# A planned attention and two-MoE kernel: transfers planned as one queue, by rows and bytes

## The chip, the cores and the metric

The kernel runs on one core of a Trainium2 chip. The metric is the device time of one execution in microseconds (us). The engines are named PE (TensorE, matmul and transposes), DVE (VectorE), ACT (ScalarE), POOL (GpSimd) and SP (SyncE, which only issues transfers here).

## What is computed

Causal attention with a gate bias over 4 batches, 8 heads, 576 positions and head size 64; then a first MoE layer (512 to 1024 to 512) with a softmax-weighted and normalized middle; then a second one (512 to 2048 to 512) with a clipped middle. There are 2304 tokens.

```python
scores = scale * np.matmul(q, k.transpose(0, 1, 3, 2))
cum = np.cumsum(np.maximum(s, 0.0), axis=-1)
bias = -(cum[:, :, :, None] - cum[:, :, None, :])
scores = np.where(causal, -1000000000.0, scores + np.minimum(bias, 0.0))
attn = softmax(scores)
x = np.matmul(attn, v)                      # heads side by side: 2304 x 512
h = x @ w_in
solu = h * softmax(h)
x = (solu - mean(solu)) / sqrt(var(solu) + 1e-06) * g_ln @ w_out
h = x @ w2_in
out = (h * np.clip(h + 3.0, 0.0, 6.0) / 6.0) @ w2_out
```

## The kernel before

All large products run on PE in a fast 32-bit form, each operand split into a high and a low part, so that one product takes three matmuls. The weights arrive as 64-bit words: a load (`raw_wi`, `raw_wo`, `rawi`, `rawo`) is decoded by ACT (`a_`: high word), by ACT or DVE (`t_`: low word) and by DVE (joined), and then split.

The attention goes by pairs of heads. For each query tile PE makes scores (L782 for the first batch, L818 later), DVE takes the maximum (L727), ACT the exponential with its row sum (L739), DVE the reciprocal, POOL scales the rows of `y` (L834, L852), PE transposes them (L886), ACT and DVE copy these into `pt` (L890), and PE multiplies with v (L913). The first MoE goes by tiles of 128 tokens (L1018, L1087, L1108) and stores its output in memory. The second MoE is a Strassen-like scheme: 24 units (3 token blocks, 8 column pairs) of seven products (L1358), whose results ACT copies into `c` (L1371) and gates with a ReLU into `g` (L1384), which is stored in memory; then nine groups of seven products (L1535) with weights `W` that are loaded into `stage` and cast (L1445) and with `r` read back (forms `fa`, `fs`, L1512). `ws` is the split form of the input weights of one unit column (L472).

No loop sets the order in which instructions stand. The functions call `plan.add(engine, us, fn, reads, writes, new, lag, ...)`, and the class `Plan` keeps a list of work. `emit` then plays it through: each engine takes, when it comes free, the ready entry that was added first (entries in the background get a rank 50 or 100 later); an entry is ready when all that it reads is written, with a hop of 0.2 or 0.3 us between engines. PSUM banks are handed out there too. The entries are then emitted in the order of their planned starts, and each engine runs its own in just that order, whatever happens.

A transfer is an entry of SP, ACT or POOL that lasts as long as its issue; what it writes counts as ready `lag` later, a number by kind: 2.0 us for decoded weights on SP, 4.0 for those that ACT issues, 4.5 for `g`, 2.5 for `W`, 3.0 for `xr`, and so on. However many transfers are on their way, each has its own lag. After the first batch `plan.spare` adds a cushion to each planned duration: 0.03 us on DVE, 0.05 on ACT, none on POOL.

Of the kernel before, what the change touches and what calls it, by code (L numbers as in the profile page):

```python
# [41 lines left out]
TRIO = 3  # L42
X_RAW = 2
HOP_TO_PE, HOP_FROM_PE, HOP = 0.3, 0.2, 0.2


class Plan:


    def __init__(self):  # L50
        self.ops, self.writers, self.users, self.rings, self.born, self.reuse = [], {}, {}, {}, {}, []
        self.takes, self.bank = {}, {}
        self.stage, self.stages = "", {}
# [43 lines left out]
    def emit(self):  # L97
# [20 lines left out]
        for i, o in enumerate(self.ops):  # L118
# [3 lines left out]
            if not waits[i]:  # L122
                heapq.heappush(pending[o[0]], (0.0, i))
        order, port_free = [], 0.0
        while len(order) < n:
# [19 lines left out]
            if i in self.takes:  # L145
# [51 lines left out]
def kernel(ctx, tc, q, k, v, s, w_in, w_out, g_ln, w2_in, w2_out, out):  # L197
    nc = tc.nc
# [80 lines left out]
    def gate_rows():  # L279
# [37 lines left out]
        for i in range(len(blocks)):  # L317
            plan.add("ACT" if i >= 2 else "SP", 0.45, lambda i=i: load(i), writes=[f"s/{i}"], lag=2.0)
        plan.add("DVE", 0.55, lambda: nc.vector.memset(one, 1.0), writes=["one"])
# [8 lines left out]
        def to_dram():  # L328
            plan.add("POOL", 0.6, lambda: nc.gpsimd.tensor_scalar(neg, first_t["cum"][: 2 * NH].bitcast(F32), -1.0, 1.0, ALU.mult, ALU.mult), reads=["gate/h", "gate/l1"], writes=["neg"])
            for x in range(2):  # L330
                r = blocks[x]
                for i, row, src, keys in ((0, 2 * x, lambda r: one[:NH], ["one"]), (1, 2 * x + 1, lambda r: one[:NH], ["one"]), (1, 2 * x, lambda r: first_t["cum"][r].bitcast(F32), ["gate/h", "gate/l1"]), (0, 2 * x + 1, lambda r: neg[r], ["neg"])):
                    plan.add("SP", 0.45, lambda i=i, row=row, src=src, r=r: put(i, row, src(r)), reads=keys, writes=[f"rows/{i}{row}"], lag=4.0)

# [12 lines left out]
    def split64(plan, pool, src, hi, lo, name, key, scale=None, bufs=1, ring="", raws64=2, after=(), hi_dve=False, on_dve=(), on_act=(), behind=None, needs=(), home=()):  # L347
# [44 lines left out]
        def put_lo():  # L392
# [3 lines left out]
            else:  # L396
# [22 lines left out]
    def decoded(pool_at, x, k, tags, ready):  # L419
# [6 lines left out]
        def block(o):  # L426
# [54 lines left out]
    def second_w2(k, pool_at, tags, stage, ready=None):  # L481
# [4 lines left out]
        def whole(i, q):  # L486
            def go():
                nc.sync.dma_start(out=wt_d[i, :, k], in_=quarters()[q])

            return lambda: plan.add("SP", 0.6, go, reads=[both[q // 2]], writes=[f"wt{k}/{i}"], lag=3.0)  # L490

        def parts(i, m, q, tag):
# [9 lines left out]
            return part(at, lambda x: T[key][:, :, x, :], key, new=[(tag[1], 1, key)], alloc=alloc) + [  # L502
                lambda: plan.add("SP", 0.6, store, reads=[f"{key}/{x}{at[0]}" for x in "hl"], writes=[f"wt{k}/{i}"], lag=4.0)]

# [61 lines left out]
    def load_qk(p):  # L566
# [7 lines left out]
        for name, src in (("q", q), ("k", k)):  # L574
# [4 lines left out]
            elif p == X_RAW:  # L579
                new, room = ([("x", 2, "x0")], []) if name == "q" else ([], ["x0/raw"])  # L580
            plan.add("SP", 1.1, lambda name=name, src=src: rows(name, src), reads=room, writes=[key], new=new, lag=4.0)

# [4 lines left out]
    def load_v(p, a=1):  # L587
# [11 lines left out]
        for j in range(2):  # L599
            plan.add("SP", 0.5 + 0.5 * a, lambda j=j: values(j), writes=[f"{key}/{j}"], new=[("V", 2, key)] if j == 0 else [], lag=3.0, after=[begun(p)])  # L600

# [51 lines left out]
    def prep_qk(p, name):  # L653
# [47 lines left out]
        def to_stack(j):  # L701
            if p == NPAIR and name == "q":
                plan.add("POOL", 1.3, lambda j=j: zeros(j), writes=[f"stack{j}/"], new=[(f"stack{j}", 1, f"stack{j}")])
            s_key = f"S{p}_{j}"
            plan.add("SP", 1.26, lambda j=j: stack(j), reads=[f"{hl_key}/{x}{c0}" for x in "hl" for c0, _ in groups] + [f"stack{j}/"],
                     writes=[f"{s_key}/{name}"], new=[(f"S{j}", 1, s_key)] if name == "q" else [], lag=3.0)
            if name == "k":
                plan.add("SP", 0.45, lambda j=j: gates(j), reads=ROWS_D + [f"stack{j}/"], writes=[f"{s_key}/g"], lag=2.0)

# [392 lines left out]
    def ffn1_out(c, m):  # L1102
# [18 lines left out]
        plan.add("ACT", act(256), put, reads=[key], writes=[f"so{key}/"])  # L1121
        plan.add("SP", 0.5, store, reads=[f"so{key}/"], writes=[f"x2_{c}_{m}"], lag=2.0)

# [72 lines left out]
    to_dram()  # L1196
    plan.add("SP", 0.5, lambda: nc.sync.dma_start(out=g_sb, in_=g_ln.rearrange("(c p) -> p c", p=P)), writes=["g"], lag=2.0, after=["HL0k/h0"])
    for b, share in enumerate(SHARES):
        main = []
        if b == 0:  # L1200
# [72 lines left out]
    def load_x(bi, lows):  # L1273
# [72 lines left out]
    def unit(bi, k):  # L1346
# [32 lines left out]
        def gate(o, h, src_key, src, eng="DVE"):  # L1379
# [44 lines left out]
    def weights(j):  # L1424
# [4 lines left out]
        for q, (k0, k1) in enumerate(PIECES):  # L1429
# [25 lines left out]
            if i in SPLIT:  # L1455
                r.append(lambda both=both, key=key, k0=k0, k1=k1, number=number: plan.add(
                    "SP", 0.0032 * 2 * P * (k1 - k0), both, reads=[f"wt{k}/{WT_PART[i]}" for k in range(k0, k1)], writes=[f"{key}/h", f"{key}/l"], new=[(f"rm{number}", 1, key)], lag=2.5))
                continue
            r += [
                lambda load=load, key=key, k0=k0, k1=k1, first=["stage"] * (number == 0), ring=[("xr", 1, "stage")] * (number == 0) + [(f"stage{home}" if home in (0, 1) else home, 1, f"{key}s")]: plan.add(  # L1460
                    "SP", 0.0016 * 2 * P * (k1 - k0), load, reads=[f"wt{k}/{WT_PART[i]}" for k in range(k0, k1)], writes=[f"{key}s", *first], new=ring, after=["stage"], lag=2.5),
                lambda high=high, key=key, n=n, number=number: plan.add("ACT", act(n), high, reads=[f"{key}s"], writes=[f"{key}/h"], new=[(f"rm{number}", 1, key)]),
# [9 lines left out]
    def group(bi, t):  # L1472
# [16 lines left out]
        def load(x, h, o):  # L1489
# [3 lines left out]

            return lambda: plan.add("SP", 1.6, go, reads=[f"gd{bi}_{h}{o}/{k}" for k in range(NK)] + (["forms"] if mine[x] == 4 else []), writes=[key(x)], new=raw_new(x), lag=3.5)

# [52 lines left out]
        def put(b, h, o, kept):  # L1548
# [10 lines left out]
            def store():  # L1559
# [90 lines left out]
```

## Time and profile before

| what | value |
|---|---|
| median of 3 runs | 799.75 us (799.14 to 799.86) |
| the profiled execution | 798.7 us, of it span 796.9 us |
| PE busy | 771.1 us (97%) |
| DVE, ACT, POOL busy | 595.1 us, 478.2 us, 228.3 us |
| DMA | 136.33 MB, mean 171 GB/s |

The span runs from the first to the last instruction. A busy share says how long an engine had an instruction in it; in a row of waits stands how long an engine stood idle before a group of instructions and what ended it. In a timeline each row is an instruction or a run of equal ones, with the idle time ahead of it in brackets. Line numbers are those of the kernel before.

### The profile page before, as it was taken

How to read it: one execution, taken by the hardware profiler on the slowest of the kernel's cores; microseconds unless marked ns; L12 is line 12 of the kernel's file. 1: busy time of each engine (PE TensorE's matmuls, PEld its weight loads, DVE VectorE, ACT ScalarE, POOL GpSimd, SP SyncE). 2: the span in 40 equal slices, each digit the busy share in tenths (PEclk: the TensorE clock that was granted, in tenths of full speed). 3: DMA queues.
4: the chain of work that ended last, by engine and by line, in shares of the span. 5: the costliest groups of instructions: out<-in, count | busy, mean ns of one | idle time of the engine just before them, and what ended most of it. 6: DMA issues, size and time to landing. Idle time of an engine off the chain costs nothing.

```text
span 796.9 us, 15897 instructions
## 1 busy us (share of the span) xinstructions
PE 771.1 (97%) x5560; PEld 707.0 (89%) x5560; DVE 595.1 (75%) x1381; ACT 478.2 (60%) x1071; POOL 228.3 (29%) x320
## 2 busy tenths in 40 slices
PE   6889999999999999999999999999997999999997
PEld 5566888888898988888989999999997999999997
DVE  5767988778957688657798898888876876666662
ACT  5877987757765667656374665666664444444441
POOL 3575454436642455251210000000032002222221
PEclk9879999999999999999999999999999999999999
DMA  8856688777757776613433545666599444444440
GB/s 204 204 141 160 162 208 202 196 195 198 169 171 194 212 170 157 187 51 139 142 107 108 183 166 175 211 218 234 167 294 412 152 140 133 131 134 131 132 128 27
DMA packets 157615, 136.33 MB, mean 171 GB/s; under 512 B 67616, under 2 KB 135200, under 8 KB 157536
## 3 DMA queue, kind: packets, MB, share of 16 engines
q1 hardware_dynamic: 153600, 122.07, 53.6%
q10 hardware_dynamic: 2400, 8.54, 3.4%
q0 software_dynamic: 1536, 4.72, 1.5%
q8 instruction: 44, 0.72, 0.4%
q14 instruction: 35, 0.29, 0.1%
HBM read 74.67 MB, written 39.39 MB: 143 GB/s over the span
## 4 chain that ended last, share of the span: by engine, by line
PE 80%; DMA 7%; DVE 6%; ACT 3%; issue 2%; POOL 1%; SPq 1%; DVEq 0%; ACTq 0%; POOLq 0%
PE bank L1535 23%; PE bank L1358 18%; PE bank L1108 10%; PE bank L1018 8%; PE bank L913 6%; PE bank L886 5%; PE bank L818 5%; PE bank L782 2%; DMA stage<-wt_d 2%; DMA rawo<-in_moe_w_out_dram 2%; DMA xr<-x_d 2%; PE bank L1087 1%; PE bank L667 1%; DMA rawi<-in_moe_w_in_dram 1%; DMA raw_wi<-in_moe_w_in_dram 1%
## 5 line engine op out<-in xcount | busy, mean ns | idle before, releaser
L1358 PE MATMUL bank<-xb,ws 128*128 128x384 f32 x1008 | 178.1, 337 | 4.5 <-ACT c L1371 3.4
L1358 PEld LDWEIGHTS bank<-xb,ws 128*128 128x128 f32 x1008 | 175.1, 188 | 6.2 <-ACT c L1371 4.6
L1535 PE MATMUL bank<-W,fs 128*128 128x256 f32 x864 | 106.3, 282 | 0.3 <-ACT c L1544 0.3
L1535 PEld LDWEIGHTS bank<-W,fs 128*128 128x128 f32 x864 | 104.3, 190 | 0.6 <-ACT c L1544 0.5
L834 POOL TENSOR_SCALAR y<-y,rsum 128x128 f32<-128x128 f32 (+4 forms) x120 | 72.5, 623 | 98.2 <-DVE rsum L830 84.9
L727 DVE CUSTOM_DVE_ANT_0 y<-bank,mask 96x288 f32<-96x288 f32 (+4 forms) x168 | 74.2, 466 | 26.2 <-PE bank L818 21.4
L739 ACT ACTIVATE y<-y,nmax 128x128 f32<-128x128 f32 (+4 forms) x140 | 83.1, 595 | 14.4 <-DVE nmax L727 7.2
L1108 PE MATMUL bank<-zh,w_out_h 128*128 128x256 f32 x288 | 83.1, 289 | 0.7 <-DVE zl L1094 0.7
L1535 PE MATMUL bank<-W,fa 128*128 128x256 f32 x648 | 81.2, 282 | 2.0 <-ACT fa L1512 1.5
L1535 PEld LDWEIGHTS bank<-W,fa 128*128 128x128 f32 x648 | 78.9, 190 | 2.6 <-ACT fa L1512 1.7
L1108 PE MATMUL bank<-zh,w_out_l 128*128 128x256 f32 x288 | 81.0, 281 | 0.0
L1108 PE MATMUL bank<-zl,w_out_h 128*128 128x256 f32 x288 | 80.9, 281 | 0.0
L1392 POOL DMA_DIRECT2D g_d<-g x24 | 13.2, 551 | 189.0 <-DVE g L1387 189.0
L1018 PE MATMUL bank<-w_in_h,xh 128*128 128x512 f32 x144 | 60.2, 418 | 0.0
L818 PE MATMUL bank<-stack 128*96 128x288 f32 (+4 forms) x288 | 58.6, 318 | 0.0
L1108 PEld LDWEIGHTS bank<-zh,w_out_h 128*128 128x128 f32 x288 | 54.2, 188 | 2.7 <-DVE zl L1094 1.2
L1018 PE MATMUL bank<-w_in_h,xl 128*128 128x512 f32 x144 | 56.6, 393 | 0.0
L1018 PE MATMUL bank<-w_in_l,xh 128*128 128x512 f32 x144 | 56.4, 392 | 0.0
L1512 ACT CAST fs<-r 128x1024 fp32r<-128x1024 f32 x27 | 28.4, 1050 | 44.8 <-PE bank L1535 27.7
L1108 PEld LDWEIGHTS bank<-zh,w_out_l 128*128 128x128 f32 x288 | 54.3, 188 | 0.4
L886 PE MATMUL bank<-ident,y 128*128 128x128 f32 (+2 forms) x420 | 52.3, 265 | 2.3 <-POOL y L852 2.3
L1108 PEld LDWEIGHTS bank<-zl,w_out_h 128*128 128x128 f32 x288 | 54.3, 188 | 0.0
(275 smaller groups left out, 1575.7 us busy)
## 6 DMA issues: line engine op xcount, KB each, us to landing
r<-g_d SPq DMA_DIRECT2D x36, 512.0 KB
g_d<-g SPq DMA_DIRECT2D x72, 192.0 KB
rawo<-in_moe_w_out_dram SPq DMA_DIRECT2D x16, 512.0 KB
rawi<-in_moe_w_in_dram SPq DMA_DIRECT2D x16, 512.0 KB
x_d<-x2s SPq DMA_DIRECT2D x36, 128.0 KB
xr<-x_d SPq DMA_DIRECT2D x6, 768.0 KB
g_d<-g POOLq DMA_DIRECT2D x24, 192.0 KB, 5.5
W<-wp_d SPq DMA_DIRECT2D x6, 768.0 KB
```

The costliest lines, as they stand in the source:

```text
L727: nc.vector.tensor_tensor_reduce(out=ys[h, t][:n, c0:c1], in0=bank(key)[:n, : c1 - c0], in1=mask[:n, 480 + n - w + c0 : 480 + n - w + c1], ...
L739: nc.scalar.activation(out=y[:n], in_=y[:n], func=AF.Exp, bias=nmax[:n, h, t : t + 1], scale=-1.0, accum_out=sums[:n, h, t : t + 1])
L782: nc.tensor.matmul(bank(keys[j])[:n, : c1 - c0], lhsT=a, rhs=b, start=(m == 0), stop=(m == 3))
L818: nc.tensor.matmul(bank(key)[:n, : c1 - c0], lhsT=ss[:, 2 - 2 * m, ST[t] : w], rhs=ss[:, 3 - 2 * m, c0:c1], start=(m == 0), stop=(m == 1))
L834: nc.gpsimd.tensor_scalar(ys[h, t][:n], ys[h, t][:n], rsum[:n, h, t : t + 1], 1.0, ALU.mult, ALU.mult)
L886: nc.tensor.transpose(bank(key)[: SZ[jj], c : c + SZ[t]], ys[h, t][: SZ[t], ST[jj] : ST[jj] + SZ[jj]], ident[: SZ[t], : SZ[t]])
L913: nc.tensor.matmul(bank(key)[j * D : (j + 1) * D, lo - c0 : c1 - c0], lhsT=vs[v_key(p, a)][:n, jj, j, :], rhs=pts[pt_key(2 * p + j, a)][:n ...
L1018: nc.tensor.matmul(bank(key), lhsT=xs[i][m // 2][:, kk, :], rhs=(w_in_l if m == 1 else w_in_h)[:, kk, f * 512 : (f + 1) * 512], start=(kk ...
L1108: nc.tensor.matmul(bank(key)[:, : 2 * P], lhsT=w_out_at(w, kk)[:, m * P : (m + 1) * P], rhs=z[:, kk, :], start=(kk == 0 and i == 0), stop= ...
L1358: nc.tensor.matmul(bank(key)[:, :W], lhsT=T[f"ws{k}"][:, WS_OF[op], a, kc * P : (kc + 1) * P], rhs=x_form(bi, op)[:, b, kc, :], start=(fir ...
L1512: nc.scalar.copy(T[name][:, 0], T[key(src)])
L1535: nc.tensor.matmul(bank(b_key)[:, : 2 * P], lhsT=T[name][:, y, k, :], rhs=T[f"W{i}_{q}"][:, k - k0, w, :], start=first and k == 0 and y == ...
```

## The change

The list gets a model of one queue in which all transfers stand. An entry may carry `dma`, the time that its transfer holds the queue, in place of `lag`; it is worked out from the number of rows (pieces in memory) and their size. In `emit` a transfer begins 1.3 us after its issue has ended, or when the one before it is through, whichever is later; it holds the queue for `dma`, and what it writes is ready 0.3 us after that. All three issuing engines share the one queue. The cushion after the first batch goes from 0.03 and 0.05 us to 0.01 and 0.02. Line numbers below L44 rise by 1, later by 9.

```diff
+DMA_START, DMA_END = 1.3, 0.3
...
-            us, lag = self.ops[i][1], self.ops[i][4]
+            us, landed = self.ops[i][1], self.ops[i][4]
...
             free[e] = end = start + us
+            if self.dma[i]:
+                dma_free = max(end + DMA_START, dma_free) + self.dma[i]
+                landed = dma_free + DMA_END - end
...
-                ready_at[j] = max(ready_at[j], end + lag + hop if done else start)
+                ready_at[j] = max(ready_at[j], end + landed + hop if done else start)
...
+def moved(rows, size):
+    return rows * (0.0087 + 0.0000368 * size) * 1.13 / 16
...
-                             lag=2.0 if behind is None else 4.0, after=after),
+                             dma=moved(128, 4096), after=after),
...
-            plan.spare = {"DVE": 0.03, "ACT": 0.05, "POOL": 0}
+            plan.spare = {"DVE": 0.01, "ACT": 0.02, "POOL": 0}
...
-            r.append(lambda: plan.add(ask, 0.55, store, reads=[g], port=False, writes=[f"gd{bi}_{h}{o}/{k}"], lag=4.5))
+            r.append(lambda: plan.add(ask, 0.55, store, reads=[g], port=False, writes=[f"gd{bi}_{h}{o}/{k}"], dma=moved(128, 1536)))
```

Some 20 more entries get a `dma` in place of their `lag` in the same way. No `fn` is touched, so the same instructions are emitted in another order. Three places show it; names carry the buffer's number, which says nothing.

At the end of the units of the second MoE, on ACT, before (L1384 is the ReLU of a gate, L1371 the copy of `c`, L1445 the cast of a loaded `W`):

```order
L1384 ACTIVATE g_6_10_7287<-bank_96 128x384
L1384 ACTIVATE g_6_01_7306<-c_6_7225 128x384
L1445 CAST W_2_7311<-stage 128x2x256
L1384 ACTIVATE g_7_00_7320<-c_7_7274 128x384
L1371 COPY c_7_7324<-bank_99 128x384
L1371 COPY c_7_7348<-bank_99 128x384
L1384 ACTIVATE g_7_11_7363<-c_7_7348 128x384
```

and now (L1393, L1380 and L1454 are the same lines):

```order
L1393 ACTIVATE g_6_10_7295<-bank_100 128x384
L1393 ACTIVATE g_6_01_7309<-c_6_7212 128x384
L1380 COPY c_7_7317<-bank_98 128x384
L1393 ACTIVATE g_7_00_7335<-c_7_7271 128x384
L1380 COPY c_7_7343<-bank_98 128x384
L1454 CAST W_2_7346<-stage 128x2x256
L1393 ACTIVATE g_7_11_7363<-c_7_7343 128x384
```

Both copies of `c` and the ReLU between them have moved ahead of the cast of `W_2`.

In the attention of the first batch, on ACT, before (L739 exponential, L364 issue of a weight load, L375 and L370 decoding, L890 copy of transposed rows):

```order
L739 ACTIVATE y_2_448,sums<-y_2_448,nmax 128x384
L375 ACTIVATE t_wi_1_557<-raw_wi_1_496 128x512
L370 ACTIVATE a_wi_1_560<-raw_wi_1_496 128x512
L890 COPY pt5a<-bank_95 128x384
L739 ACTIVATE y_3_286,sums<-y_3_286,nmax 96x480
L739 ACTIVATE y_4_309,sums<-y_4_309,nmax 96x576
L390 CAST w_in_h<-a_wi_1_560 128x512
L375 ACTIVATE t_wi_1_596<-raw_wi_1_549 128x512
L890 COPY pt6a<-bank_99 128x384
L364 DMA raw_wi_1_600<-in_moe_w_in_dram 128x1024
L890 COPY pt7a<-bank_100 128x384
L739 ACTIVATE y_4_310,sums<-y_4_310,nmax 96x576
```

and now (L748, L373, L384, L379, L899; these rows follow the four exponentials of `ye`):

```order
L379 ACTIVATE a_wi_0_537<-raw_wi_0_487 128x512
L384 ACTIVATE t_wi_0_545<-raw_wi_0_487 128x512
L899 COPY pt4a<-bank_99 128x384
L899 COPY pt5a<-bank_98 128x384
L748 ACTIVATE y_2_447,sums<-y_2_447,nmax 128x384
L384 ACTIVATE t_wi_1_562<-raw_wi_1_494 128x512
L373 DMA raw_wi_1_575<-in_moe_w_in_dram 128x1024
L748 ACTIVATE y_4_310,sums<-y_4_310,nmax 96x576
L899 COPY pt6a<-bank_96 128x384
L899 COPY pt7a<-bank_99 128x384
```

pt5a now stands directly behind pt4a, and the exponential y_4_310 (the last query tile of head 1) ahead of pt6a. The exponentials y_3 and y_4 of head 0 and y_3 of head 1 have gone further up. The load that a_wi_0_537 and t_wi_0_545 decode is issued at row 49 of ACT, behind two exponentials of `y_1`; before it was issued at row 43, ahead of them. On POOL one subtraction for the weights (L397) stands between the scalings of `y_3` of the two heads, as before, but it is that of an earlier weight block; the later blocks follow behind more scalings of `yl`.

At the first column pair of the second MoE, on DVE, before (L1062 scaling of `e`, L1039 its product with h and its sum, L1043 to L1051 small steps, L472 the low parts of `ws`):

```order
L1062 TENSOR_SCALAR e_5029<-e_5029,st_5028 128x1024
L1039 ISA e_5070,st_5069<-bank_99,e_5070 128x512
L1039 ISA st_5069 128x1
L1039 ISA e_5070,st_5069<-bank_97,e_5070 128x512
L1039 ISA st_5069 128x1
L1043 TENSOR_SCALAR st_5069<-st_5069 128x1
L1050 TENSOR_SCALAR st_5069<-st_5069 128x1
L1051 TENSOR_SCALAR st_5069<-st_5069 128x1
L472 TENSOR_TENSOR ws_5135<-ai_4723,ws_5135 128x2x256
L472 TENSOR_TENSOR ws_5135<-ai_4723,ws_5135 128x256
```

and now (L1071, L1038 and L1041 maximum of h, L481, L1338 to L1341 the sums of `ai`, L1048):

```order
L1071 TENSOR_SCALAR e_5026<-e_5026,st_5025 128x1024
L1038 TENSOR_REDUCE st_5069<-bank_95 128x1
L1041 TENSOR_SCALAR st_5069<-st_5069 128x1
L481 TENSOR_TENSOR ws_5136<-ai_4796,ws_5136 128x2x256
L481 TENSOR_TENSOR ws_5136<-ai_4796,ws_5136 128x256
L1338 TENSOR_TENSOR ai_4796<-ai_4796 128x256
L1339 TENSOR_TENSOR ai_4796<-ai_4796 128x256
L1340 TENSOR_TENSOR ai_4796<-ai_4796 128x256
L1341 TENSOR_TENSOR ai_4796<-ai_4796 128x256
L1048 ISA e_5070,st_5069<-bank_102,e_5070 128x512
L1048 ISA st_5069 128x1
```

The low parts of `ws` and the four sums now stand ahead of the two products of the last tile's softmax.

## Rows read from the trace of the kernel before

**Rows 1.** The page: the span, busy time by engine, and PE's granted clock in 40 slices

```profile
span 796.9 us, 15897 instructions
...
PE 771.1 (97%) x5560; PEld 707.0 (89%) x5560; DVE 595.1 (75%) x1381; ACT 478.2 (60%) x1071; POOL 228.3 (29%) x320
...
PEclk9879999999999999999999999999999999999999
```

**Rows 2.** Windows: busy us (instructions) by engine, granted PE clock, DMA share, GB/s

```profile
36.00:40.00 4.00, 2.59 (x11) 1.51 (x11) 1.33 (x2) 3.53 (x8) 2.00 (x6) 0.50 0.78 192
52.00:56.00 4.00, 4.00 (x23) 3.31 (x22) 2.30 (x6) 2.58 (x7) 4.00 (x4) 0.52 0.34 122
460.00:520.00 60.00, 60.00 (x344) 59.68 (x343) 51.39 (x105) 36.46 (x80) 0.00 (x0) 1.00 0.56 192
```

**Rows 3.** Waits of PE: total us, times, longest us

```profile
PE bank L1358 <- ACT c L1371: 3.4, 3, 2.6
PE bank L886 <- POOL y L852: 2.3, 1, 2.3
...
PE bank L1535 <- ACT fa L1512: 1.5, 1, 1.5
PE bank L913 <- ACT pt5a L890: 1.4, 1, 1.4
...
PE bank L1358 <- DVE ws L472: 1.0, 1, 1.0
...
PE bank L1108 <- DVE zl L1094: 0.7, 1, 0.7
PE bank L913 <- DVE pt L890: 0.7, 1, 0.7
```

**Rows 4.** Timeline of ACT near 605 us: start, length, instruction, idle before

```profile
602.96 0.53 ACT L1384 ACTIVATE g<-c 128x384 f32<-128x384 f32 x1 [2.54 <-DMA g_d<-g]
605.80 0.62 ACT L1445 CAST W<-stage 128x512 fp32r<-128x512 f32 x1 [2.32 <-DMA stage<-wt_d]
...
606.75 0.46 ACT L1371 COPY c<-bank 128x384 f32<-128x384 f32 x1
```

**Rows 5.** Timeline of PE, 600 to 608 us

```profile
599.82 4.15 PE L1358 MATMUL bank<-xb,ws 128*128 128x384 f32 x23
603.80 0.87 PE L1535 MATMUL bank<-W,fa 128*128 128x256 f32 x6
```

**Rows 6.** The chain that ended last: start us, us, what

```profile
29.87 6.20 DMA raw_wi<-in_moe_w_in_dram
...
598.11 7.67 DMA stage<-wt_d
```

**Rows 7.** Timeline of DVE near 409 us

```profile
408.08 0.68 DVE L1039 CUSTOM_DVE_ANT_0 e<-bank,e 128x512 f32<-128x512 f32 x1
...
409.92 1.02 DVE L472 TENSOR_TENSOR ws<-ai,ws 128x512 fp32r<-128x512 f32 x2
```

**Rows 8.** Timeline of POOL, 44 to 49 us

```profile
44.04 3.52 POOL L852 TENSOR_SCALAR y<-y,rsum 128x384 f32<-128x384 f32 x3 [3.01 <-PE bank L782]
47.54 1.26 POOL L397 TENSOR_TENSOR w_in_l<-a_wi,w_in_h 128x512 fp32r<-128x512 f32 x1
```

**Rows 9.** Timeline of ACT, 26 to 42 us

```profile
26.09 0.33 ACTq L364 DMA_DIRECT2D raw_wi<-in_moe_w_in_dram  x1
...
32.09 0.67 ACT L375 ACTIVATE t_wi<-raw_wi 128x512 int32<-128x512 uint32 x1 [0.26 <-DMA raw_wi<-in_moe_w_in_dram]
...
34.76 0.48 ACT L890 COPY pt4a<-bank 128x384 f32<-128x384 f32 x1
...
35.24 0.61 ACT L739 ACTIVATE y<-y,nmax 128x384 f32<-128x384 f32 x1
...
37.27 0.46 ACT L890 COPY pt5a<-bank 128x384 f32<-128x384 f32 x1
...
41.57 0.78 ACT L739 ACTIVATE y<-y,nmax 96x576 f32<-96x576 f32 x1
```

More of the change, by code (lines that the diff above doesn't have):

```diff
@@ L123, in emit @@
                 heapq.heappush(pending[o[0]], (0.0, i))
-        order, port_free = [], 0.0
+        order, port_free, dma_free = [], 0.0, 0.0
         while len(order) < n:
@@ L317, in gate_rows @@
         for i in range(len(blocks)):
-            plan.add("ACT" if i >= 2 else "SP", 0.45, lambda i=i: load(i), writes=[f"s/{i}"], lag=2.0)
+            plan.add("ACT" if i >= 2 else "SP", 0.45, lambda i=i: load(i), writes=[f"s/{i}"], dma=moved(32, 2304))
         plan.add("DVE", 0.55, lambda: nc.vector.memset(one, 1.0), writes=["one"])
@@ L332, in to_dram @@
                 for i, row, src, keys in ((0, 2 * x, lambda r: one[:NH], ["one"]), (1, 2 * x + 1, lambda r: one[:NH], ["one"]), (1, 2 * x, lambda r: first_t["cum"][r].bitcast(F32), ["gate/h", "gate/l1"]), (0, 2 * x + 1, lambda r: neg[r], ["neg"])):
-                    plan.add("SP", 0.45, lambda i=i, row=row, src=src, r=r: put(i, row, src(r)), reads=keys, writes=[f"rows/{i}{row}"], lag=4.0)
+                    plan.add("SP", 0.45, lambda i=i, row=row, src=src, r=r: put(i, row, src(r)), reads=keys, writes=[f"rows/{i}{row}"], dma=moved(32, 2304))
         return to_dram
@@ L449, in block @@
             for f in (
-                lambda: plan.add("SP", 1.5, load, reads=[ready] if ready else [], writes=[raw], new=[(raw_tag, 1, raw)], lag=2.0),
+                lambda: plan.add("SP", 1.5, load, reads=[ready] if ready else [], writes=[raw], new=[(raw_tag, 1, raw)], dma=moved(512, 1024) if x == "i" else moved(128, 4096)),
                 lambda: plan.add("ACT", 0.61, high, reads=[raw], writes=[f"{a_key}/{o}"], new=[(a_tag, 1, a_key)] if o == 0 else []),
@@ L488, in go @@
                 nc.sync.dma_start(out=wt_d[i, :, k], in_=quarters()[q])
-            return lambda: plan.add("SP", 0.6, go, reads=[both[q // 2]], writes=[f"wt{k}/{i}"], lag=3.0)
+            return lambda: plan.add("SP", 0.6, go, reads=[both[q // 2]], writes=[f"wt{k}/{i}"], dma=moved(128, 1024))
         def parts(i, m, q, tag):
@@ L502, in parts @@
             return part(at, lambda x: T[key][:, :, x, :], key, new=[(tag[1], 1, key)], alloc=alloc) + [
-                lambda: plan.add("SP", 0.6, store, reads=[f"{key}/{x}{at[0]}" for x in "hl"], writes=[f"wt{k}/{i}"], lag=4.0)]
+                lambda: plan.add("SP", 0.6, store, reads=[f"{key}/{x}{at[0]}" for x in "hl"], writes=[f"wt{k}/{i}"], dma=moved(128 * m, 2048))]
         def sums():
@@ L580, in load_qk @@
                 new, room = ([("x", 2, "x0")], []) if name == "q" else ([], ["x0/raw"])
-            plan.add("SP", 1.1, lambda name=name, src=src: rows(name, src), reads=room, writes=[key], new=new, lag=4.0)
+            plan.add("SP", 1.1, lambda name=name, src=src: rows(name, src), reads=room, writes=[key], new=new, dma=2 * moved(576, 256))
     def v_key(p, a):
@@ L599, in load_v @@
         for j in range(2):
-            plan.add("SP", 0.5 + 0.5 * a, lambda j=j: values(j), writes=[f"{key}/{j}"], new=[("V", 2, key)] if j == 0 else [], lag=3.0, after=[begun(p)])
+            plan.add("SP", 0.5 + 0.5 * a, lambda j=j: values(j), writes=[f"{key}/{j}"], new=[("V", 2, key)] if j == 0 else [], dma=moved(576 if a else 256, 256), after=[begun(p)])
     def first_home(p, name):
@@ L1121, in ffn1_out @@
         plan.add("ACT", act(256), put, reads=[key], writes=[f"so{key}/"])
-        plan.add("SP", 0.5, store, reads=[f"so{key}/"], writes=[f"x2_{c}_{m}"], lag=2.0)
+        plan.add("SP", 0.5, store, reads=[f"so{key}/"], writes=[f"x2_{c}_{m}"], dma=moved(128, 1024))
     def ffn1_pieces():
@@ L1196 @@
     to_dram()
-    plan.add("SP", 0.5, lambda: nc.sync.dma_start(out=g_sb, in_=g_ln.rearrange("(c p) -> p c", p=P)), writes=["g"], lag=2.0, after=["HL0k/h0"])
+    plan.add("SP", 0.5, lambda: nc.sync.dma_start(out=g_sb, in_=g_ln.rearrange("(c p) -> p c", p=P)), writes=["g"], dma=moved(1024, 4), after=["HL0k/h0"])
     for b, share in enumerate(SHARES):
@@ L1456, in weights @@
                 r.append(lambda both=both, key=key, k0=k0, k1=k1, number=number: plan.add(
-                    "SP", 0.0032 * 2 * P * (k1 - k0), both, reads=[f"wt{k}/{WT_PART[i]}" for k in range(k0, k1)], writes=[f"{key}/h", f"{key}/l"], new=[(f"rm{number}", 1, key)], lag=2.5))
+                    "SP", 0.0032 * 2 * P * (k1 - k0), both, reads=[f"wt{k}/{WT_PART[i]}" for k in range(k0, k1)], writes=[f"{key}/h", f"{key}/l"], new=[(f"rm{number}", 1, key)], dma=moved(128, 2048 * (k1 - k0))))
                 continue
@@ L1460, in weights @@
                 lambda load=load, key=key, k0=k0, k1=k1, first=["stage"] * (number == 0), ring=[("xr", 1, "stage")] * (number == 0) + [(f"stage{home}" if home in (0, 1) else home, 1, f"{key}s")]: plan.add(
-                    "SP", 0.0016 * 2 * P * (k1 - k0), load, reads=[f"wt{k}/{WT_PART[i]}" for k in range(k0, k1)], writes=[f"{key}s", *first], new=ring, after=["stage"], lag=2.5),
+                    "SP", 0.0016 * 2 * P * (k1 - k0), load, reads=[f"wt{k}/{WT_PART[i]}" for k in range(k0, k1)], writes=[f"{key}s", *first], new=ring, after=["stage"], dma=moved(128, 1024 * (k1 - k0))),
                 lambda high=high, key=key, n=n, number=number: plan.add("ACT", act(n), high, reads=[f"{key}s"], writes=[f"{key}/h"], new=[(f"rm{number}", 1, key)]),
@@ L1492, in go @@
                 nc.sync.dma_start(out=T[key(x)], in_=g_d[bi, h, o, :, :, t * P : (t + 1) * P])
-            return lambda: plan.add("SP", 1.6, go, reads=[f"gd{bi}_{h}{o}/{k}" for k in range(NK)] + (["forms"] if mine[x] == 4 else []), writes=[key(x)], new=raw_new(x), lag=3.5)
+            return lambda: plan.add("SP", 1.6, go, reads=[f"gd{bi}_{h}{o}/{k}" for k in range(NK)] + (["forms"] if mine[x] == 4 else []), writes=[key(x)], new=raw_new(x), dma=moved(1024, 512))
         def total(to, a, b, op):
```

13 lines of the change are left out of this document (7 added, 6 removed).

## The prediction

> **What bounds the kernel now.** I read the page first, then the waits of TensorE (PE), the windows, and the timelines of the stretches in which PE waits. The page gives PE as busy for 97% of the span, at full clock in all but the first slices [rows 1]. Busy alone proves little for an engine whose ends are modelled, so the windows decide: from 460 to 520 us PE works 60.00 of 60 us and weight loads fill 59.68 [rows 2]. No order shortens such a stretch. The change alters no arithmetic, so it can only give back time in which PE waits, or add some. The reader is to see how few waits there are: 3.4 us in three behind one line (the longest 2.6, so 0.8 in the other two), 2.3, 1.5, 1.4, 1.0, 0.7 and 0.7 us [rows 3]: 11 us beside a span of 796.9. That is the prize, apart from the clock, which stands near half in parts of 35 to 56 us [rows 2].
>
> The waits have one shape. PE waits for ScalarE (ACT), VectorE (DVE) or GpSimd (POOL); that engine is not slow, but at the head of its queue stands an instruction that waits for a transfer or that the planner put there too early. Every engine runs in the order that the plan wrote. So I followed each wait to the instruction ahead of the one PE needs, and looked whether the new order still has it there.
>
> **The change, part by part.** It removes and adds no operation of the computation; work, bytes and transfers stay. What moves is positions. Transfers on SP and ACT swap by a few places; an issue costs ACT 0.33 us of its sequencer wherever it stands [rows 9], and SP computes nothing, so I price a moved transfer by when its reader can start.
>
> *The end of the second MoE's first product (607 us).* PE waits 2.59 us for the copy of c, which ACT runs at 606.75 us [rows 4, 5]. Ahead of it stand the cast of W at 605.80, which waited 2.32 us for a transfer, and a gate's ReLU [rows 4]. That transfer took 7.67 us from its issue [rows 6], where the old list counted 2.5 us behind the issue. In the new order the copy stands directly behind the ReLU that ends at 602.96 + 0.53 = 603.49 us [rows 4], ahead of both. What it reads was finished by 599.82 + 4.15 = 603.97 us at the latest [rows 5], so it ends by 603.97 + 0.46 = 604.4, while PE is occupied until 603.80 + 0.87 = 604.67 us [rows 5]. Gain: 607.26 - 604.67 = 2.6 us. If the ReLU now ahead of the next copy waits for a free buffer, part comes back; if the 1.5 us wait for fa just behind also goes, more is won. I take -2.6, with ends -4.1 and 0. Late next is the cast of W itself, but many products of the second stage stand before the one that reads it.
>
> *The first ws (410 us).* PE waits 1.0 us for the low part of ws, which DVE starts at 409.92, behind the two products of the softmax that begin at 408.08 us, and three small ones [rows 3, 7]. Now ws stands ahead of the products: 409.92 - 408.08 = 1.84 us earlier, more than the wait. The four sums of ws go ahead too; the softmax that they delay feeds transposes that stand 48 products of the first MoE's output later, which cover it. Without that cover, part of the 1.0 comes back. I take -1.0, ends -1.0 and 0.
>
> *The transposes of head 0 (50 us).* PE waits 2.3 us for POOL's scaling of y [rows 3]. POOL idles 3.01 us before 44.04, runs three scalings in 3.52 us, then a weight subtraction of 1.26, then the scaling that PE needs [rows 8]. It can start only when the row sums of heads 0 and 1 are complete, and the last addend is the exponential that ACT runs at 41.57 us [rows 9]. The new order has this exponential behind pt5a, one exponential (0.61) and one t_wi (0.67): 37.27 + 0.46 + 0.61 + 0.67 = 39.0 us instead of 41.57, 2.5 us earlier [rows 9]. One weight subtraction remains between the scalings, so POOL's run keeps its length and ends 2.5 us earlier: the wait nearly vanishes. I take -2.0, ends -2.3 and 0. Cover that could be lost: POOL's last weight subtractions now stand behind more scalings, about 3.52 / 3 = 1.2 us each at most; if PE reaches the products that read them first, part of the gain comes back.
>
> *pt4a and pt5a (35 to 38 us).* PE waits 1.4 us for pt5a [rows 3], because a t_wi and an a_wi, fed by a transfer, stand ahead of it. They go behind it. But the transfer before that one, issued at 26.09 and used at 32.09 (6.0 us) [rows 9], is now issued behind two exponentials, about 29.4 to 29.9 us, and its a_wi and t_wi still stand ahead of pt4a. At 6.0 us they begin at 35.4 to 35.9, and two of 0.67 us later, near 37.0, pt4a follows, where it ran at 34.76; pt5a near 37.5, where it ran at 37.27 [rows 9]. PE does the same products in one piece. I take 0; the ends are -1.4 (the transfer lands in time) and +1.0 (PE does pt4a's share, which was done before, behind it). *A rule speaks against the change here.* Its formula puts every transfer in one queue and gives this load 1.13 x 128 x (0.0087 + 0.0000368 x 4096) / 16 = 1.44 us, plus 1.3 and 0.3 around it and 0.35 of issue: 3.4 us. Two such loads on ACT's queue took 6.0 and 6.20 us [rows 6, 9]. The Trainium skill, "DMA: Bandwidth & Descriptors", section "Queues, rings and completion order", says that each DMA engine takes turns between the queues that have work, packet by packet, so a load issued on ACT shares with all that SP issues after it and is not served before it. The trace agrees with the rule here.
>
> *The other waits* (0.7, 0.7 and the 0.8) [rows 3]: 2.2 us. Behind them stand transfers that the old list counted too short (2.0 us behind the issue for 512 KB, now 3.0); I credit half, -1.1, ends -2.2 and 0.
>
> *The cushion.* From the second batch on each DVE instruction is planned 0.02 us shorter and each ACT one 0.03. No row shows what waits a new order adds. The nearest: beside the starts up to 56 us and the three places above, the old one left those 2.2 us. I charge about half of them, +1.0, with ends 0 and +4, about twice them.
>
> Sum: -2.6 - 1.0 - 2.0 + 0 - 1.1 + 1.0 = -5.7 us. The profiled execution took 798.7 us, 796.9 of it span [rows 1], and lies 1.05 under the median of 799.75. So 793.0 for such an execution and 794.1 us as a median. All low ends together give -11.0, all high ends +5.0.
>
> **The rivals.** *Slower, by the cushion.* The place is the 24 units of the second MoE's first product, where DVE is busy 51.39 of 60 us [rows 2]. Planned tighter, copies of c come just behind the product that needs their bank. The price of one such wait is some 0.4 us, the two short ones of line 1358 [rows 3]. One in each unit costs 9.6 us: 799.75 - 6.7 (the sum without its +1.0) + 9.6 = 802.7 us. It decides from 17 of the 24 units on, where it eats the gain. For it: PE has no slack there. Against: ACT is busy only 36.46 of 60 us [rows 2], and the longest wait there came from a transfer.
>
> *No change.* Places swap and waits reappear elsewhere, as any new order has some: 799.75. For it speaks that 11 us in 797 is little. Against: three of the waits have a named instruction ahead that is gone.
>
> *The model of one queue is wrong for ACT's loads*, so the change does not do what it says. By rows (6.0 us against a planned 3.4), a_wi and t_wi hold the head of ACT's queue for about 2 us with exponentials behind them; the 2.0 us at 50 us is lost and the high end of +1.0 at 37 us added: 794.1 + 2.0 + 1.0 = 797.1 us. It is the mechanism that the skill's rule of turns describes.
>
> *The clock.* PE's clock is 0.50 in 36 to 40 us and 0.52 in 52 to 56, both beside waits; PE was busy 2.59 and 4.00 us there [rows 2]. At full clock half of it is saved: 794.1 - 3.3 = 790.8 us, and some more where the half clock reaches beyond these windows. Against it: ACT is busy 3.53 of 4 us in the first [rows 2], so PE would still wait there.
>
> **How the numbers follow.** Forecast 0.45, ACT's loads 0.12, the clock 0.13, no change 0.13, slower 0.17. A measurement of this kernel tells about 0.2% (1.6 us) from no change. Faster: 0.45, 0.13 and most of 0.12, less the forecast's upper tail: 0.67; same 0.16; slower 0.17. The range reaches down past the clock's case to 788, most of the way to the low ends, and up past no change with its scatter to 801.5; little lies below, the slower rival above, together 2 in 10.
>
> **What would show it.** Right: the wait of 2.6 us for c gone and PE closed from 600 to 610 us; no wait for ws at 410; POOL's scalings from about 41.5 us. The fault with ACT's loads would show as ACT idle ahead of a_wi at 33 to 36 us; the slower rival as many short waits for c between 410 and 610. The forecast is wrong if PE is no further on at 60 us than before, or if its waits add up to 11 us again.

## The result, and the profile after

The changed kernel takes **792.63 us** (median of 9 runs, 789.25 to 796.0), the kernel before 799.14 us beside it (9 runs, 797.41 to 800.6). The ratio is 0.9919, with a 95% interval of 0.9898 to 0.9940: 0.8% faster. The forecast was 794.1 us. The profiled execution took 793.27 us.

The page of the changed kernel, lines that answer to [rows 1]:

```profile
span 791.4 us, 15889 instructions
PE 769.7 (97%) x5560; PEld 706.4 (89%) x5560; DVE 595.1 (75%) x1381; ACT 476.3 (60%) x1071; POOL 228.2 (29%) x320
PEclk9989999999999999999999999999999999999999
```

The span fell by 5.5 us. What lies outside PE's busy time went from 796.9 - 771.1 = 25.8 to 791.4 - 769.7 = 21.7 us, so 4.1 us of the gain are idle time and 1.4 are busy time, on the same matmuls. The waits of PE in the changed kernel (total us, times, longest) answer to [rows 3]:

```profile
PE bank L636 <- DMA rawq<-in_q_dram: 5.1, 1, 5.1
PE bank L1544 <- ACT c L1553: 2.0, 3, 1.1
PE bank L1544 <- ACT fa L1521: 1.5, 1, 1.5
PE bank L922 <- ACT pt4a L899: 1.3, 1, 1.3
PE bank L827 <- DMA x_d<-x2s: 1.2, 1, 1.2
PE bank L895 <- DVE nmax L736: 1.1, 2, 0.8
PE bank L895 <- DVE pt4b L899: 1.0, 1, 1.0
PE bank L827 <- DVE HL6q L688: 0.8, 1, 0.8
PE bank L636 <- DMA rawk<-in_k_dram: 0.7, 1, 0.7
...
PE bank L895 <- POOL y L861: 0.5, 1, 0.5
PE bank L1367 <- DVE ws L481: 0.4, 1, 0.4
...
PE bank L1117 <- DVE zl L1103: 0.2, 1, 0.2
```

Five waits of the kernel before that the forecast left out of its 11 us, from the same view of it:

```profile
PE bank L627 <- DMA rawq<-in_q_dram: 5.6, 2, 5.3
...
PE bank L667 <- DMA rawk<-in_k_dram: 1.8, 1, 1.8
...
PE bank L782 <- DVE nmax L727: 1.2, 2, 0.7
...
PE bank L627 <- DMA rawk<-in_k_dram: 1.0, 1, 1.0
PE bank L1535 <- ACT c L1544: 0.8, 2, 0.5
```

The reader sees that no wait for a copy of `c` is left in the first product of the second MoE (L1358, now L1367; 3.4 us before), that the 2.3 us for POOL's `y` are 0.5, and that new names have come: `x_d`, `HL6q`, `pt4b`. All rows of the view add up to 22.2 us before and 17.8 now; without those for `rawq` and `rawk` at the start, to 13.8 and 12.0.

How far PE was at 60 us, before and now (busy us, matmuls, granted clock, DMA share, GB/s):

```profile
0.00:60.00 60.00, 45.92 (x295) 0.89 0.76 183
```

```profile
0.00:60.00 60.00, 49.68 (x351) 0.94 0.76 193
```

PE's timeline gives the split by stage (start, length, instruction, idle before), before at the start of the second MoE's first product, and now:

```profile
409.32 0.34 PE L1358 MATMUL bank<-xb,ws 128*128 128x384 f32 x1
```

```profile
407.81 2.25 PE L1367 MATMUL bank<-xb,ws 128*128 128x384 f32 x12
...
617.79 3.10 PE L1544 MATMUL bank<-W,fs 128*128 128x256 f32 x24 [1.09 <-ACT c L1553]
```

So 1.5 us of the 5.5 are won ahead of that product and 4.0 behind it. The lead of the start is larger and does not last: the first scores of the second batch (L818, now L827) begin at 74.40 us where they began at 82.42, and of these 8.0 us only 1.5 are left at 407.81.

### The profile page after: what moved, and what is told of

It is laid out like the page before. It is cut to its first block, busy times and chain, and to the rows that moved or that the text cites. A ratio compares the mean times of both kernels' runs of the same rounds, so it can differ in the third digit from the quotient of the medians.

```text
span 791.4 us, 15889 instructions
## 1 busy us (share of the span) xinstructions
PE 769.7 (97%) x5560; PEld 706.4 (89%) x5560; DVE 595.1 (75%) x1381; ACT 476.3 (60%) x1071; POOL 228.2 (29%) x320
## 4 chain that ended last, share of the span: by engine, by line
PE 87%; DVE 5%; DMA 3%; ACT 2%; SPq 1%; issue 1%; POOL 0%; ACTq 0%; DVEq 0%; POOLq 0%
PE bank L1367 22%; PE bank L1544 22%; PE bank L1027 12%; PE bank L1117 12%; PE bank L922 6%; PE bank L827 5%; PE bank L895 5%; PE bank L1096 2%; PE bank L676 1%; PE bank L791 1%; DMA raw_wo<-in_moe_w_out_dram 1%; DMA raw_wi<-in_moe_w_in_dram 1%; DMA s_sb<-in_s_dram 1%; DVE y L736 1%; ACT y L748 1%
## 5 line engine op out<-in xcount | busy, mean ns | idle before, releaser
L1367 PE MATMUL bank<-xb,ws 128*128 128x384 f32 x1008 | 177.0, 336 | 0.4 <-DVE ws L481 0.4
L1367 PEld LDWEIGHTS bank<-xb,ws 128*128 128x128 f32 x1008 | 175.4, 188 | 0.7 <-DVE ws L481 0.7
L748 ACT ACTIVATE y<-y,nmax 128x384 f32<-128x384 f32 (+4 forms) x140 | 83.2, 596 | 15.4 <-DVE nmax L736 11.3
L827 PE MATMUL bank<-stack 128*96 128x288 f32 (+4 forms) x288 | 58.6, 318 | 2.3 <-DMA x_d<-x2s 1.2
```

Source lines behind the costliest of these rows:

```text
L748: nc.scalar.activation(out=y[:n], in_=y[:n], func=AF.Exp, bias=nmax[:n, h, t : t + 1], scale=-1.0, accum_out=sums[:n, h, t : t + 1])
L827: nc.tensor.matmul(bank(key)[:n, : c1 - c0], lhsT=ss[:, 2 - 2 * m, ST[t] : w], rhs=ss[:, 3 - 2 * m, c0:c1], start=(m == 0), stop=(m == 1))
L1367: nc.tensor.matmul(bank(key)[:, :W], lhsT=T[f"ws{k}"][:, WS_OF[op], a, kc * P : (kc + 1) * P], rhs=x_form(bi, op)[:, b, kc, :], start=(fir ...
```

## The experiments

All kernels compute the same; only the plan's numbers, and which entries use the queue, differ. Ratios are to runs of the kernel before on the same chip.

| run | latencies | cushion DVE, ACT | median us | ratio (95%) |
|---|---|---|---|---|
| the change | one queue | 0.01, 0.02 | 792.63 | 0.9919 (0.9898 to 0.9940) |
| cushion_alone | fixed | 0.01, 0.02 | 812.51 | 1.0177 (1.0148 to 1.0205) |
| queue_alone | one queue | 0.03, 0.05 | 794.27 | 0.9952 (0.9932 to 0.9972) |
| queue_no_cushion | one queue | 0, 0 | 790.63 | 0.9909 (0.9886 to 0.9933) |
| queue_first_batch | one queue, fixed after the first batch | 0.01, 0.02 | 804.89 | 1.0089 (1.0061 to 1.0117) |
| queue_later | fixed, one queue after the first batch | 0.01, 0.02 | 797.27 | 0.9979 (0.9960 to 0.9998) |
| long_lags | fixed, four of them longer | 0.01, 0.02 | 800.88 | 1.0045 (1.0026 to 1.0063) |
| act_loads_apart | one queue but for ACT's loads | 0.01, 0.02 | 793.36 | 0.9934 (0.9907 to 0.9961) |
| act_apart_no_cushion | the same | 0, 0 | 790.87 | 0.9900 (0.9864 to 0.9936) |
| hop_before | fixed, hop 0.32 | 0.03, 0.05 | 805.18 | 1.0082 (1.0050 to 1.0114) |
| hop28_before | fixed, hop 0.28 | 0.03, 0.05 | 802.71 | 1.0049 (1.0024 to 1.0074) |
| hop_after | one queue, hop 0.32 | 0.01, 0.02 | 791.41 | 0.9916 (0.9889 to 0.9942) |
| hop28_after | one queue, hop 0.28 | 0.01, 0.02 | 797.97 | 0.9990 (0.9965 to 1.0016) |

**Queue or cushion.** The two parts of the change, each alone. cushion_alone is the kernel before with

```diff
-            plan.spare = {"DVE": 0.03, "ACT": 0.05, "POOL": 0}
+            plan.spare = {"DVE": 0.01, "ACT": 0.02, "POOL": 0}
```

> The kernel before with only the smaller cushion (0.01 on DVE, 0.02 on ACT); the fixed latencies stay. My theory: the gain is the queue model's and the cushion costs up to 1.0 us, so 799.1 to 800.2 us, with the waits for c near 607 us and for ws near 410 us still there (the order up to some 75 us is the one of before, so the waits for y at 50 us and for pt5a at 38 us too). Rival, the cushion is what gives: 793 to 796 us. Rival, any new order falls as it happens: anywhere from 795 to 804 us, with waits at new places.

It took 812.51 us, far above every number that was expected. Two of its waits of PE:

```profile
PE bank L1358 <- ACT c L1371: 5.3, 5, 1.9
...
PE bank L818 <- ACT pt L890: 2.6, 1, 2.6
```

and ACT's timeline ahead of the 2.6 us (310 us) and of one of 1.85 us (468 us):

```profile
309.33 0.66 ACT L439 ACTIVATE ao<-rawo 128x512 f32<-128x512 f32 x1 [3.42 <-DMA rawo<-in_moe_w_out_dram]
309.90 0.47 ACT L890 COPY pt<-bank 128x384 f32<-128x384 f32 x1
...
464.98 0.84 ACT L1297 CAST xb<-xr 128x768 fp32r<-128x768 f32 x1 [1.97 <-DMA xr<-x_d]
465.72 0.52 ACT L1384 ACTIVATE g<-c 128x384 f32<-128x384 f32 x1
466.15 1.55 ACT L1297 CAST xb<-xr 128x768 fp32r<-128x768 f32 x2
467.60 0.85 ACT L1371 COPY c<-bank 128x384 f32<-128x384 f32 x2
```

It is the shape of [rows 4]: the reader of a load that the plan thinks landed (2.0 us for `rawo`, 3.0 for `xr`) stands at the head of ACT's queue, and the copy that PE needs stands behind it. With fixed latencies, then, the larger cushion seems to have kept most of these readers back; long_lags tests that below. The waits shown are only part of the loss. Of the 15.5 us by which the span grew, 13.0 are lost ahead of the second MoE:

```profile
422.34 1.90 PE L1358 MATMUL bank<-xb,ws 128*128 128x384 f32 x10
```

From 100 to 400 us PE idles 7.9 us where it idled 1.4, and does 2126 matmuls where it did 2223. What makes its busy time slower there, the traces do not tell.

queue_alone is the changed kernel with the old cushion.

> The changed kernel with the old cushion (0.03 and 0.05). My theory: the queue model's part alone, 791.6 to 793 us, the first 75 us as in the changed kernel, no wait over 1 us for c of the first product near 600 us and none for ws at 408 us. Rival, the cushion is what gives: about 797 us, since only the start would be better. Rival, any new order falls as it happens: 790 to 798 us.

It took 794.27 us, 1.3 us above my theory's range and inside that of the second rival; no wait for c or ws is left in the first product, as expected. The queue alone gives 0.5%, the smaller cushion on top of it some 0.3% more by the medians; the intervals of the two overlap, so that second step is not shown. The smaller cushion is worth nothing or a little gain with the queue, and costs 1.8% without it.

**Which part of the plan.** An entry got both numbers, and a switch at the end of the first batch chose:

```diff
-        self.dma.append(dma)
+        self.dma.append(dma if self.one_queue else 0.0)
```

> The changed kernel, but entries added after the first batch have their old fixed latency again; the small cushion stays. My theory now (a fixed latency that is too short puts the reader of a load at the head of ACT's queue, and the cushion of before covered just that; the one queue makes it needless): the first 75 us as in the changed kernel, then the losses of the run with the smaller cushion alone, 803 to 811 us, with waits of 1.5 us and more for c in 440 to 480 us. Rival, the better start carries through: 793 to 797 us.

> The changed kernel, but the first batch has its old fixed latencies; one queue and the small cushion after it. My theory: the start of before (7 to 8 us later at the first MoE's first product), of which the attention gives back most, and the second MoE as in the changed kernel: 793 to 796 us. Rival, the start is the gain: 798 to 800 us.

Measured were 804.89 and 797.27 us: the first as my theory had it, the second 1.3 us above its range (and below the rival's). Against cushion_alone the queue in the first batch is worth 0.9% of the time before (1.0177 - 1.0089), the queue behind it 2.0% (1.0177 - 0.9979), both 2.6%. Against the kernel before, with its larger cushion, it reads otherwise: with the first batch planned as before only 0.2% of the 0.8% is left, and the intervals (0.9960 to 0.9998, 0.9898 to 0.9940) do not overlap. Most of the gain over that kernel thus needs the new order of the first batch. In queue_first_batch PE waits 2.7 us for `c` between 440 and 480 us, the longest 1.9; in queue_later it waits 2.3 us for POOL's `y` again, as in [rows 3]. All traces agree on `c`: the longest wait for it in the first product is 1.5 to 2.8 us in the six kernels with fixed latencies behind the first batch, and at most 0.5 in the eight with the queue there, whatever the cushion or the hop.

**Mean latency or queue.** long_lags is cushion_alone with four longer numbers (`rawi` and `rawo`, `xr`, the two kinds of `W`):

```diff
-..., new=[(raw_tag, 1, raw)], lag=2.0)
+..., new=[(raw_tag, 1, raw)], lag=3.4)
...
-..., lag=3.0))
+..., lag=4.2))
...
-..., new=[(f"rm{number}", 1, key)], lag=2.5))
+..., new=[(f"rm{number}", 1, key)], lag=5.7))
...
-..., after=["stage"], lag=2.5),
+..., after=["stage"], lag=3.1),
```

> The kernel before with the smaller cushion and no queue, but with the four latencies that are too short set to what the trace of before shows as their mean: 3.4 us in place of 2.0 for decoded weights on SP, 4.2 in place of 3.0 for xr, 5.7 in place of 2.5 for W that is loaded whole, 3.1 in place of 2.5 for stage. Theory A, what counts is that the mean latency is right: 793 to 797 us, no wait over 1 us for pt near 310 us or for c in 440 to 480 us. Theory B, the latency must follow what else is in the queue: 802 to 811 us.

800.88 us lies between the two theories. Four numbers take back 1.3% (1.0177 - 1.0045): no wait for `pt` near 310 us, none for `c` between 440 and 480. What the mean can't do is seen in long_lags' ACT timeline at 605 us, its PE timeline, and its chain of waits:

```profile
605.10 0.62 ACT L1445 CAST W<-stage 128x512 fp32r<-128x512 f32 x1 [4.94 <-DMA stage<-wt_d]
605.62 0.93 ACT L1384 ACTIVATE g<-c 128x384 f32<-128x384 f32 x2
606.46 0.46 ACT L1371 COPY c<-bank 128x384 f32<-128x384 f32 x1
```

```profile
606.97 2.29 PE L1358 MATMUL bank<-xb,ws 128*128 128x384 f32 x6 [2.81 <-ACT c L1371]
```

```profile
597.45 7.62 DMA stage<-wt_d
```

It is the wait of [rows 4 to 6] again. A load of this kind that was given 3.1 us behind its issue takes 7.62 from the issue's start here: SP issues it at 597.45 us and four loads of whole `W` from 597.86 us on, right behind it, before it lands. A latency that follows what else is on its way can keep its cast back: in the changed kernel, with as tight a cushion, the wait is gone. That a larger number for this one load would do the same was not tried.

**ACT's loads.** In act_loads_apart the loads on ACT's queue have a latency of their own:

```diff
-                             dma=moved(128, 4096), after=after),
+                             **({"dma": moved(128, 4096)} if behind is None else {"lag": 5.0}), after=after),
```

> The changed kernel, but the loads that ACT issues (raw_wi, raw_wo) stand outside the one queue, with a latency of their own of 5.0 us behind the issue (in the trace of the changed kernel one of them took 5.32 us on the chain, where the queue counts 3.4 from the issue's start). Theory A, the queue is wrong for these loads and that costs the start some time: PE's wait for pt4a near 35 us (1.3 us) gone or under 0.6, 789.5 to 791.5 us. Theory B, it is wrong and hidden: 791.5 to 794 us. Rival, the queue model earns the start just by counting these loads short: 795 us and more.

793.36 us, as theory B. ACT no longer waits for this load, and `pt4a` is still copied at 34.90 us, now because PE delivers late:

```profile
31.80 0.64 ACT L384 ACTIVATE t_wi<-raw_wi 128x512 int32<-128x512 uint32 x1
...
34.90 0.48 ACT L899 COPY pt4a<-bank 128x384 f32<-128x384 f32 x1 [0.92 <-PE bank L895]
```

In the waits of PE a new one of 1.7 us stands in its place:

```profile
PE bank L676 <- DMA rawq<-in_q_dram: 1.7, 1, 1.7
```

**No cushion.** queue_no_cushion has zeros in `plan.spare`; act_apart_no_cushion joins it with the edit above.

> The changed kernel without any cushion (0 and 0). My theory: with one queue the cushion covers nothing that matters, so 791 to 794.5 us. Rival, the slower case of the prediction, copies of c planned just behind their product cost a short wait of 0.4 us in many of the 24 units: 797 us and more.

> The same, and no cushion either: the two single edits that looked best together. If both gains add: 787.5 to 790 us. If the rest is the scatter of orders: 790 to 793.5 us, no better than the changed kernel without cushion.

790.63 us (0.4 below my theory's range) and 790.87 us, the second no better than the first. Neither has a wait for `c` in the first product, so the rival of many short waits falls with a cushion of nothing at all. Both beat the kernel before; neither can be told from the change, whose interval overlaps theirs. If these two edits had gains of their own, they don't add.

**A new order alone.** One edit without a meaning, in both kernels: the planned hop to PE is 0.32 or 0.28 us in place of 0.30.

```diff
-HOP_TO_PE, HOP_FROM_PE, HOP = 0.3, 0.2, 0.2
+HOP_TO_PE, HOP_FROM_PE, HOP = 0.32, 0.2, 0.2
```

> The kernel before with an edit that means nothing: the planned hop to PE is 0.32 us in place of 0.30. It reorders about as many instructions as the change does. It measures how far the time moves by a new order alone. My theory (the latencies of the model are what matters): 798 to 801 us. Rival, any new order falls as it happens: 3 us or more away from 799.1 us, on either side; then one order that is 6.5 us better shows little of the model.

> The changed kernel with the same edit that means nothing (planned hop to PE 0.32 us in place of 0.30). My theory: 791 to 794.5 us, within 2 us of the change. Rival, any new order falls as it happens: 3 us or more away from 792.6 us, some of the gain gone.

> The kernel before with the planned hop to PE at 0.28 us in place of 0.30, an edit that means nothing. With fixed latencies a new order was up to 14 us worse, and never better. If the order of before is a lucky one among such orders: 801 to 808 us. If the order with a hop of 0.32 us was the exception: 797 to 800 us.

> The changed kernel with the same edit. If the one queue makes the plan insensitive to such edits: 790 to 794.5 us. If 792.6 us was as lucky as the order of before: 797 us and more.

The kernel before got 0.8% and 0.5% slower, so its order was a good one among its like: my theory that the latencies alone count missed hop_before by 4 us. The changed kernel stayed with 0.32, but lost nearly all its gain with 0.28, the case that I had called as lucky as the order of before: there PE waits once for a gate row of a stack, whose transfer is issued at 131.84 us and lands 3.02 us later. This one wait is about half of the 5.3 us lost; the rest was not traced to a cause.

```profile
135.02 0.76 PE L827 MATMUL bank<-stack 128*96 128x288 f32 x2 [2.79 <-DMA stack<-rows_d]
```

So a new order alone moves the time by up to some 6.5 us, and a single pair of kernels proves little about a model. Over the three hops the fixed latencies with their larger cushion have ratios of 1, 1.0082 and 1.0049 (mean 1.0044), the one queue with the smaller one 0.9919, 0.9916 and 0.9990 (mean 0.9942). At each hop the queue is the faster, by 0.6 to 1.7%. Three orders are few, and the size of the mean gain (1.0%) stays rough; its sign does not rest on one order.

## Why the prediction was right

The time, the sign and the three named waits came out as forecast. That the sum fits so well is luck. By the view of waits what it credited came to -7.6 us in place of -6.7, and the new waits to +5.8 in place of +1.0: together -1.8 us, not -5.7. What makes up for it stood at nothing in the sum: 2.6 us of waits at the start and 1.4 us of PE's busy time. Of its two signs of being wrong the first did not come (351 matmuls by 60 us, 295 before), but the second did: without `rawq` and `rawk` the waits add up to 12.0 us, in other places.

*The end of the first product (607 us): right, with part given back.* The copy stands ahead of the cast, as the ACT timeline of the changed kernel shows:

```profile
601.75 0.48 ACT L1380 COPY c<-bank 128x384 f32<-128x384 f32 x1 [1.71 <-PE bank L1367]
602.13 0.63 ACT L1454 CAST W<-stage 128x512 fp32r<-128x512 f32 x1
...
616.41 1.04 ACT L1521 CAST fs<-r 128x1024 fp32r<-128x1024 f32 x1 [3.90 <-DVE r L1509]
617.36 0.38 ACT L1553 ACTIVATE c<-bank 128x256 f32<-128x256 f32 x1
```

All 3.4 us of waits for `c` in the first product are gone. But in the second product they rose from 0.8 to 2.0 us: at 617.36 a copy stands behind a cast that waits for DVE. The 1.5 us for `fa` stayed. From 600 to 640 us PE is busy 36.83 us where it was 35.62. The sign "PE closed from 600 to 610 us" failed, then, by the 1.5 us for `fa` at 607.

*The first ws: right.* DVE's timeline has the low parts ahead of the products, and PE enters the first product without a wait; 0.4 us came back at another `ws`.

```profile
404.19 1.02 DVE L481 TENSOR_TENSOR ws<-ai,ws 128x512 fp32r<-128x512 f32 x2
...
406.96 0.68 DVE L1048 CUSTOM_DVE_ANT_0 e<-bank,e 128x512 f32<-128x512 f32 x1
```

*POOL's scalings: right, and earlier than forecast* (41.5 us). POOL's timeline:

```profile
37.63 2.86 POOL L861 TENSOR_SCALAR y<-y,rsum 128x384 f32<-128x384 f32 x4 [0.66 <-DVE rsum L857]
...
41.95 1.63 POOL L861 TENSOR_SCALAR y<-y,rsum 96x576 f32<-96x576 f32 x2
```

The wait of 2.3 us at 50 us is gone; the 0.5 us of the view is another one, at 32.58 us, so 1.8 of the 2.0 are won. Late next, and not named by me, is DVE's maximum, 0.8 us.

*pt4a and pt5a: right at 0, by other steps.* One wait took the other's place: 1.4 us for `pt5a` before, 1.3 for `pt4a` now. But the load on ACT's queue was issued at 27.71 us, not at 29.4 to 29.9, so `pt4a` follows at 34.24 and not near 37.0. As the rival said, it landed later than planned and ACT idled ahead of `a_wi` (the chain of waits, then ACT's timeline):

```profile
27.71 5.32 DMA raw_wi<-in_moe_w_in_dram
```

```profile
33.11 0.67 ACT L379 ACTIVATE a_wi<-raw_wi 128x512 f32<-128x512 f32 x1 [0.73 <-DMA raw_wi<-in_moe_w_in_dram]
...
34.24 0.46 ACT L899 COPY pt4a<-bank 128x384 f32<-128x384 f32 x1
```

5.32 us stand against 3.4 for this load alone in the planned queue. The Trainium skill, "DMA: Bandwidth & Descriptors", section "Queues, rings and completion order", has each DMA engine take turns between queues; for this load the trace shows little of it, since from 29.5 to 31.5 us ACT's queue moved 0.57 MB and SP's 0.01. ACT issued a second such load at 28.33 us, and by 33.1 us its queue had moved 1.00 MB, nearly the bytes of both. The price of the rival was wrong: 0.73 us of ACT's idle time, not 2, and act_loads_apart shows no gain from counting such loads longer (5.0 us behind the issue).

*The other waits: larger than the half that I credited.* `pt` and `zl` went from 1.4 to 0.2 us together, and the two short ones for `c` are gone.

*The cushion and new waits: mis-sized, and the cause was another.* The term was +1.0 us, with an end at +4. New waits cost about 5.8 us: 2.3 behind L827, 1.2 for `c` in the second product, 1.0 for `pt4b`, 0.5 for `x`, and 0.4 each more for `nmax` and for the first operands of the scores. They come from the new order, most of them behind 77 us, and not from the cushion: with the queue a smaller cushion costs nothing. Where the smaller cushion does cost, without the queue, it costs 14 us, most of it ahead of the second MoE; the waits that the timelines explain are few and long (2.6 us for `pt`, up to 1.9 for `c`) behind late transfers, not many of 0.4. The slower rival had the mechanism wrong, and its place was safe for a reason that I hadn't seen: the cushion stood in for latencies that were too short.

*What the sum left out made up for it.* Waits for `rawk` fell by 2.1 us and that for `rawq` by 0.5 at the start, and PE was busy 1.4 us less. That the order did this for `rawk` is not shown: cushion_alone, with PE's order of before up to 98 us, waits 1.0 us for it and not 2.8. By the view of waits: -3.4 (`c`) - 1.8 (`y`) - 0.6 (`pt3a` to `pt5a`) - 0.6 (`ws`) - 1.2 (`pt`, `zl`) - 2.6 (`rawk`, `rawq`) + 5.8 = -4.4 us.

*The clock: a part of that rival came, at nothing in the sum.* The granted clock is 0.50 from 35.4 to 42.2 and from 49.0 to 55.8 us before, and from 43.1 to 49.9 us now; the mean is 0.991 and 0.995. How much of the gain this is, no run separates, but it may be the larger part. Four executions of each kernel, on several chips, had nearly the same mean clock: 0.996 before, 0.995 to 0.997 now. Their medians are 795.9 and 793.8 us, 2.1 us apart and not 6.5. And queue_later, which keeps 0.2 of the 0.8%, has clocks of 0.989 to 0.994, like most executions of the kernel before.

## What to carry to other kernels

In a planned order a latency that is too short does its harm on the engine that reads the load: it puts the reader at the head of an in-order queue, with work behind it that the bottleneck needs. Longer numbers fixed most of that here; for a burst, where one transfer took 7.6 us and the plan counted 3.1, a model of what else is on its way did; and a cushion that seems to be slack may be standing in for such an error, so remove it together with the error. Before a gain of 1% is put down to a model, change a number that means nothing: here that alone moved the time by up to 0.8%. Compare the granted clocks too before a gain is put down to waits.

## What the runs showed of the hardware

The granted clock of PE differs between executions of one order. Nine executions of the changed kernel: five had a mean granted clock of 1.000 and spans of 787.4 to 791.5 us, four had 0.995 to 0.997 and 790.6 to 794.0. In 65 executions of the kernel before, on three chips, it was never above 0.996. Two kernels with the same order of PE until past the first scores of the second batch, the changed one and queue_first_batch, show the place. The windows of the changed kernel (columns as in [rows 2]):

```profile
40.00:44.00 4.00, 2.64 (x19) 1.58 (x19) 3.96 (x9) 3.82 (x10) 3.80 (x5) 0.88 0.80 210
44.00:48.00 4.00, 3.71 (x21) 3.71 (x22) 3.78 (x14) 2.84 (x6) 2.37 (x3) 0.50 0.48 132
48.00:52.00 4.00, 4.00 (x15) 3.16 (x14) 3.21 (x10) 2.91 (x7) 2.98 (x4) 0.76 0.51 138
```

and of queue_first_batch:

```profile
40.00:44.00 4.00, 2.38 (x19) 1.29 (x15) 4.00 (x10) 3.67 (x10) 4.00 (x5) 1.00 0.82 211
44.00:48.00 4.00, 3.76 (x27) 3.07 (x28) 4.00 (x15) 3.19 (x7) 2.66 (x3) 1.00 0.50 147
48.00:52.00 4.00, 4.00 (x26) 2.58 (x26) 3.02 (x8) 2.37 (x5) 2.98 (x4) 1.00 0.54 151
```

PE was busy 2.64 and 2.38 of the 4 us from 40 to 44 us. In one the clock then fell to 0.50 (1.2 GHz, the lower of its two levels) and PE did 21 matmuls in 44 to 48 us; in the other it stayed at 1.00 (2.4 GHz) and PE did 27. The first scores of the second batch follow at 74.4 and 72.1 us. What decides between the two was not tried and stays open.
